# Two decoder layers over four batches: the second layer's V tiles all loaded after the next batch's first layer, and the GLU products cut in quarters

## Chip, cores and metric

The kernel runs on one core of a Trainium2 chip. The metric is the device time of one execution in microseconds (us). Eleven executions of the kernel before are given, and one more was taken with the profiler.

## The reference

The program computes the same two blocks twice, with the same weights and the same caches: an attention block over a cached K and V, and a gated feed-forward block (GLU). Four batches (b = 0 to 3) hold one query token each.

```python
# B=4, Sq=1, D=512; Hq=32 query heads, Hkv=8 cached heads, Sk=4096, Dh=128; F=1792
def _A_ref(x, k_cache, v_cache, wq, wo):
    q = (x @ wq) as heads; k, v = caches, each head used by 4 query heads
    p = softmax(q @ k^T * Dh ** -0.5)
    return (p @ v) @ wo
def _B_ref(x, w_gate, w_up, w_down):
    return (sigmoid(x @ w_gate) * (x @ w_up)) @ w_down

x = A_x
x = x + _A_ref(_layernorm(x), A_k_cache, A_v_cache, A_wq, A_wo)      # layer 0
x = x + _B_ref(_layernorm(x), B_w_gate, B_w_up, B_w_down)
x = x + _A_ref(_layernorm(x), A_k_cache, A_v_cache, A_wq, A_wo)      # layer 1
x = x + _B_ref(_layernorm(x), B_w_gate, B_w_up, B_w_down)
```

All tensors are bf16. The caches are 33.6 MB each. K is read from memory once, for both layers; V is read twice, once for each layer.

## The kernel before

**Tiles and slots.** A cached head of one batch comes as two tiles of 512 KB, q = 0 and q = 1. `K(b)` is 16 tiles, `V0(b)` the 16 tiles of V as layer 0 reads them, `V1(b)` the same 16 tiles read again for layer 1. They share a ring of 22 slots (`NS`), `ring0` to `ring21`. A V tile is free again when its 16 matmuls (`values`, O_ps) are done. A K tile stays for longer: it is transposed in place (`transpose_k`, VectorE), read by the scores of layer 0 and, after the whole feed-forward block of that batch, by the scores of layer 1. So 16 slots are held by a batch's K until layer 1's scores are done, and 6 slots carry everything else. The weights lie in their own space and are loaded once.

**Order of loads.** SyncE (SP) issues all loads in the order of the code, each when its slot is free. After batch 0's loads, it goes batch by batch, and here stands the number that the change touches:

```python
    pre = 3
    for b in range(1, B):
        for g in range(pre):
            load_v(1, b - 1, g)          # 6 tiles of V1(b-1)
        load_k(b, 0)                     # 16 tiles of K(b), in two halves
        load_k(b, 1)
        for g in range(8):
            load_v(0, b, g)              # 16 tiles of V0(b)
        for g in range(pre, 8):
            load_v(1, b - 1, g)          # the other 10 tiles of V1(b-1)
```

At the end come the 16 tiles of V1(3).

**Order of the work.** `_Sched` is a list scheduler that runs when the kernel is built. Each operation is put with an engine, an estimated duration and a priority; `place()` plays the program through with these estimates, fixes the order of each engine's instructions and gives each load the ring slot that is free earliest in that plan. On the chip each engine then follows its fixed order and waits on semaphores, and each load waits for the former user of its fixed slot.

The flow of a batch: `scores` (S_ps) and `softmax` of layer 0, in two halves s = 0, 1 of 16 query heads; `values` with V0(b) and the projection `y_proj` (Y_ps from oT and wo); `cross(0, b)`; then the queries of layer 1 (`q_proj`, M_ps from xT and wq, and `q_spread`, which writes the `qbd` tile); `scores` and `softmax` of layer 1, and after these those of layer 0 for batch b+1. `values` of V1(b-1) are put beside this.

`cross` is the feed-forward block: residual add (`xj`), layer norm, products with `wu` (Y_ps) and `wg` (G_ps), 56 matmuls each, tanh, the `hT` product, 56 matmuls with `wd`, residual add, layer norm for the next attention. `stat` is a matmul with a constant column that sums over partitions; `rstd` is such a `stat` followed by a VectorE step (L433) and a power on GpSimd (L437) that gives the scale that tanh needs. In the kernel before, `rstd` is put after all 56 `wg` matmuls. In layer 1 all four batches go through one common `cross(1, None)` at the very end.

Of the kernel before, what the change touches and what calls it, by code (L numbers as in the profile page):

```python
# [197 lines left out]
def bass_interleave_layers__gqa_block_cached__glu_gated_glu__decode_kernel(nc, A_x, A_k, A_v, A_wq, A_wo, B_x, B_wg, B_wu, B_wd, out):  # L198
# [5 lines left out]
    P = 128  # L204
    KD = D // P
# [13 lines left out]
    S = _Sched(NS)  # L219
# [3 lines left out]
    def sb(name, shape, dtype=dt.float32):  # L223
        return es.enter_context(nc.sbuf_tensor(name, list(shape), dtype))
# [9 lines left out]
    wg = sb("wg", [P, KD, F], bf)  # L234
    wu = sb("wu", [P, KD, F], bf)
    NF = F // P
# [15 lines left out]
    rs_h = cols[:, 20:24]  # L252
# [19 lines left out]
    nb = tr  # L272
# [24 lines left out]
    def mm(o, l, r, start=True, stop=True):  # L297
        return lambda e: e.matmul(o, lhsT=l, rhs=r, start=start, stop=stop)  # L298
# [61 lines left out]
    def load_wd():  # L360
        load_w("wd", wd[:], B_wd.rearrange("(c p) n -> p c n", p=P), P * NF * D * 2)
# [13 lines left out]
        load_v(0, 0, g)  # L375
    load_w("wu", wu[:], B_wu.rearrange("(k p) n -> p k n", p=P), P * KD * F * 2)
    load_wd()
    pre = 3
    for b in range(1, B):
        for g in range(pre):  # L380
            load_v(1, b - 1, g)
# [10 lines left out]
    def bcast(ap, m):  # L392
        return ap.unsqueeze(2).broadcast_to([P, ap.shape[1], m])

    def stat(c, si, nb, w, wkey, prio):
        S.put(
            "pe", mm(G_ps[:, c:c + nb], col(w), xsum[:, si:si + nb]), 0.58, prio, reads=[f"xsum{si}", wkey], writes=["G"],
        )
# [31 lines left out]
    def rstd(mult, rs, rs_key, nb, prio):  # L430
        stat(4, 4, nb, pos, "pos", prio)
        S.put(
            "dve", lambda e: e.tensor_scalar(vpe[:, 0:nb], G_ps[:, 4:4 + nb], mult, mult * eps, op0=ALU.mult, op1=ALU.add),  # L433
            0.17, prio, reads=["G"], writes=["vpe"],
        )
        S.put(
            "pool", lambda e: e.tensor_tensor(rs, vpe[:, 0:nb], mhalf[:, 0:nb], ALU.pow), 0.6, prio,  # L437
            reads=["vpe", "mhalf"], writes=[rs_key],
        )
# [122 lines left out]
        return pi  # L562

    def values(l, b, s, pi, prio, gis=range(4)):
        for gi in gis:
            for q in range(2):
                tile = V[l, b, 4 * s + gi, q]
                fns = []
                for t in range(q * HT, (q + 1) * HT):
                    def fn(e, t=t, gi=gi, tile=tile):  # L570
                        return e.matmul(  # L571
                            O_ps[:, gi * R:(gi + 1) * R], lhsT=ring[tile.slot][:, (t % HT) * DH:(t % HT + 1) * DH],
                            rhs=pt_sb[pi][:, t % 4, t // 4, gi, :], start=t == 0, stop=t == T - 1,
                        )
                    fns.append(fn)
                S.put("pe", fns, 0.57, prio, reads=[f"pt{pi}"], writes=["O"], tiles=[tile])
        c0, c1 = gis[0] * R, (gis[-1] + 1) * R
        o = (oT1[:] if l == 0 else oT2[:, :, b])[:, 16 * s + c0:16 * s + c1]
        S.put(
            "dve", lambda e: e.tensor_tensor(o, O_ps[:, c0:c1], winv[pi][:, c0:c1], ALU.mult), 0.2, prio - 1.5,  # L580
            reads=["O", f"winv{pi}"], writes=[f"oT{l}{s}{gi}" for gi in gis],
        )
# [14 lines left out]
    def cross(l, b, prio):  # L597

        last = l == 1
        nb = B if last else 1  # L600
        xres = xj[:] if last else x0[:, b, :]
        y = Y_ps[:, 0:nb * KD]
        u = Y_ps[:, 64:64 + NF * nb]
        g = G_ps[:, 64:64 + NF * nb]
        rs = rs_h[:, 0:nb]
        if last:
            x, xkey, xt = xj[:], "xj", xTj
            S.put(
                "dve", lambda e: e.tensor_tensor(xj[:], y.rearrange("p (b k) -> p b k", b=nb), xj[:], ALU.add), 0.2, prio,
                reads=["Y", "xj"], writes=["xj"],  # L610
            )
            layer_norm(x, xkey, xTj[:], "xTj", nb, prio)
            xk, xtkey = (lambda k: xTj[:, :, k]), "xTj"
        else:
            x, xkey = xj[:, b, :], "xj"
            S.put(
                "dve", lambda e: e.scalar_tensor_tensor(
                    out=x, in0=y, scalar=1.0, in1=xres, op0=ALU.mult, op1=ALU.add, accum_out=xsum[:, 0:1],
                ), 0.3, prio, reads=["Y", "x0"], writes=["xj", "xsum0"],
            )  # L620
            layer_norm(x, xkey, xT[:], "xT", 1, prio)
            xk, xtkey = (lambda k: xT[:, k:k + 1]), "xT"
        for w, key, dst, bkey in ((wg, "wg", g, "G"), (wu, "wu", u, "Y")):
            fns = []
            for f in range(NF):
                for k in range(KD):
                    fns.append(mm(
                        dst[:, f * nb:(f + 1) * nb], w[:, k, f * P:(f + 1) * P], xk(k), k == 0, k == KD - 1,
                    ))
            S.put("pe", fns, 1.85, prio, reads=[xtkey, key], writes=[bkey])  # L630
            if w is wg:
                rstd(4.0, rs, "rs_h", nb, prio)
        if last:
            S.put(
                "dve", lambda e: e.tensor_tensor(
                    gs[:].rearrange("p (f b) -> p f b", b=nb), g.rearrange("p (f b) -> p f b", b=nb),
                    rs.unsqueeze(1).broadcast_to([P, NF, nb]), ALU.mult
                ), 0.2, prio, reads=["G", "rs_h"], writes=["gs"],
            )
            S.put("act", lambda e: e.activation(gs[:], gs[:], ACTF.Tanh), 0.25, prio, reads=["gs"], writes=["gs"])  # L640
        else:
            S.put(
                "act", lambda e: e.activation(gs[:, 0:NF], g, ACTF.Tanh, scale=rs), 0.22, prio, reads=["G", "rs_h"],
                writes=["gs"],
            )
        S.put(
            "dve", lambda e: e.scalar_tensor_tensor(
                out=hT[:, 0:NF * nb], in0=gs[:, 0:NF * nb], scalar=1.0, in1=u, op0=ALU.add, op1=ALU.mult
            ), 0.2, prio, reads=["gs", "Y"], writes=["hT"],
        )  # L650
        fns = []
        for j in range(KD):
            for f in range(NF):
                fns.append(mm(
                    y.rearrange("p (b k) -> p b k", b=nb)[:, :, j], wd[:, f, j * P:(j + 1) * P],
                    hT[:, f * nb:(f + 1) * nb], f == 0, f == NF - 1,
                ))
        S.put("pe", fns, 1.85, prio, reads=["hT", "wd"], writes=["Y"])
        if not last:
            S.put(  # L660
                "dve", lambda e: e.scalar_tensor_tensor(
                    out=x, in0=y, scalar=rs, in1=x, op0=ALU.mult, op1=ALU.add, accum_out=xsum[:, 0:1],
                ), 0.3, prio, reads=["Y", "rs_h", "xj"], writes=["xj", "xsum0"],
            )
            layer_norm(x, xkey, xT[:], "xT", 1, prio)
            rstd(float(DH), rs_q[1][:, b:b + 1], f"rs_q1{b}", 1, prio)
            return
        S.put(
            "dve", lambda e: e.tensor_tensor(
                xw[:], y.rearrange("p (b k) -> p b k", b=nb), bcast(rs, KD), ALU.mult  # L670
            ), 0.2, prio, reads=["Y", "rs_h"], writes=["xw"],
        )
        S.put("dve", lambda e: e.tensor_tensor(xTj[:], xw[:], xj[:], ALU.add), 0.17, prio, reads=["xw", "xj"], writes=["xTj"])
        S.put(
            "pe", mm(M_ps[0:16, 0:P], xTj[:].rearrange("p b k -> p (b k)"), ident_b[:]), 0.3, prio, reads=["xTj", "ident_b"],
            writes=["M"],
        )
        S.put("dve", lambda e: e.tensor_copy(x16[0:16, :], M_ps[0:16, 0:P]), 0.2, prio, reads=["M"], writes=["x16"])
        S.put(
            "act", lambda e: e.dma_start(out.rearrange("b o (k p) -> (b o k) p", k=KD), x16[0:16, :]), 0.4, prio,  # L680
            reads=["x16"], writes=["out"], dma="out",
        )
# [12 lines left out]
    def attend(l, b, s, prio, u=None):  # L695
# [12 lines left out]
        writes=["x0"],  # L708
# [5 lines left out]
    for s in range(NH):  # L714
        fns = []
# [37 lines left out]
    for s in range(NH):  # L753
        for gis in (range(0, 3), range(3, 4)):
            values(1, B - 1, s, pis[1, B - 1, s], PV, gis)
            y_proj(1, s, PX, gis)
    cross(1, None, PX)
    S.put("sp", lambda e: None, 0.1, 0, reads=["out"])

# [39 lines left out]
```

## Time and profile before

| | us |
|---|---|
| median of 11 runs (lowest, highest) | 348.74 (345.34, 351.06) |
| the profiled execution, its own time | 348.01 |
| its span in the profile | 345.7 |
| TensorE busy (matmuls / weight loads) | 220.2 / 169.5 |
| VectorE busy | 138.5 |
| ScalarE busy | 52.8 |
| read from memory, mean over the span | 114.56 MB, 331 GB/s |
| granted TensorE clock, mean | 0.68 |

The span is the part of the execution between first and last instruction; 2.3 us lie around it. The profiled execution is 0.7 us below the median. Busy shares are means over stages that have different limits, so the stages have to be looked at one by one: the table of 40 slices on the page shows where the loads run at full rate and where they don't.

### The profile page before, as it was taken

To read this page: it belongs to the slowest core of one execution; us is meant where nothing else is said; L and a number is where in the kernel's file an instruction comes from. 1 tells how busy PE (TensorE), PEld (TensorE's weight loads), DVE (VectorE), ACT (ScalarE), POOL (GpSimd) and SP (SyncE) were. 2 spreads that over 40 slices of the span, in tenths; PEclk is the share of its full clock that TensorE was granted. 3 is DMA by queue.
4 is the path that set the end of the run, shared out by engine and by line. 5 is a ranking of instruction groups with operands and counts; after the bars stand their busy time and mean duration, and the time that the engine had idled before them with its cause. 6 is when DMAs were issued, how large, how long until landed. Compare 5 with 4: busy or idle time off the path is not lost.

```text
span 345.7 us, 11881 instructions
## 1 busy us (share of the span) xinstructions
PE 220.2 (64%) x5426; PEld 169.5 (49%) x5426; DVE 138.5 (40%) x341; ACT 52.8 (15%) x128; POOL 10.5 (3%) x38
## 2 busy tenths in 40 slices
PE   1322861265877568685856587786774686777876
PEld 1202551155635147675433366684351476763765
DVE  3777610000189951101579920011899501015111
ACT  1003030000033203000240320000333020002300
POOL 5000000000000000000000000000000000000001
PEclk9999999999985555555675555555855555558755
DMA  7999999999489999999499999967899999986900
GB/s 264 372 401 410 409 342 367 409 399 377 179 292 407 407 409 367 359 379 309 149 342 383 413 391 335 398 226 297 310 414 410 409 345 370 349 325 218 388 8 2
DMA packets 36897, 115.32 MB, mean 334 GB/s; under 512 B 3312, under 2 KB 9200, under 8 KB 36848
## 3 DMA queue, kind: packets, MB, share of 16 engines
q1 hardware_dynamic: 36816, 114.57, 88.1%
q8 instruction: 42, 0.69, 0.8%
q14 instruction: 7, 0.06, 0.0%
q10 hardware_dynamic: 32, 0.00, 0.0%
HBM read 114.56 MB, written 0.00 MB: 331 GB/s over the span
## 4 chain that ended last, share of the span: by engine, by line
DMA 41%; PE 27%; issue 14%; DVE 10%; SPq 7%; POOLq 0%; ACT 0%; DVEq 0%
DMA ring<-in_A_v_cache_dram 31%; PE S_ps L488 7%; PE O_ps L571 6%; PE M_ps L298 5%; PE Y_ps L298 5%; DMA wd<-in_B_w_down_dram 5%; SPq L331 5%; DVE ring L475 4%; PE G_ps L298 3%; DMA wo<-in_A_wo_dram 3%; DMA ring<-in_A_k_cache_dram 2%; SPq L347 2%; DVE ml L504 2%; DVE qbd L466 1%; PE PT_ps L298 1%
## 5 line engine op out<-in xcount | busy, mean ns | idle before, releaser
L571 PE MATMUL O_ps<-pt_sb,ring 128*128 128x4 bf16 x2048 | 67.1, 167 | 40.5 <-DMA ring<-in_A_v_cache_dram 32.0
L571 PEld LDWEIGHTS O_ps<-pt_sb,ring 128*128 128x128 bf16 x2048 | 63.5, 105 | 48.6 <-DMA ring<-in_A_v_cache_dram 22.0
L475 DVE STREAM_TRANSPOSE ring<-ring 128x1024 int32<-128x1024 int32 x64 | 75.8, 1216 | 9.9 <-DMA ring<-in_A_k_cache_dram 9.6
L488 PE MATMUL S_ps<-ring,qbd 128*16 128x512 bf16 x512 | 54.7, 580 | 11.8 <-DVE ring L475 11.8
L528 ACT ACTIVATE p_sb<-S_ps,cols 128x512 bf16<-128x512 f32 x32 | 24.6, 772 | 94.1 <-DVE cols L523 94.1
L504 DVE TENSOR_REDUCE ml<-S_ps 128x1 f32<-128x512 f32 x32 | 21.6, 673 | 37.6 <-PE S_ps L488 37.6
L580 DVE TENSOR_TENSOR oT<-O_ps,winv 128x12 bf16<-128x12 f32 (+2 forms) x29 | 4.9, 168 | 70.7 <-PE O_ps L571 70.4
L488 PEld LDWEIGHTS S_ps<-ring,qbd 128*16 128x16 bf16 x512 | 13.3, 109 | 33.5 <-issue 16.7
L298 PE MATMUL Y_ps<-oT,wo 128*128 128x1 bf16 (+1 forms) x640 | 20.3, 166 | 9.3 <-DVE oT L580 5.7
L298 PE MATMUL PT_ps<-ident_b,p_sb 128*128 128x64 bf16 x128 | 10.7, 225 | 21.4 <-ACT p_sb L528 21.2
L298 PEld LDWEIGHTS Y_ps<-oT,wo 128*128 128x128 bf16 x640 | 18.6, 104 | 11.6 <-DVE oT L580 7.0
L298 PEld LDWEIGHTS PT_ps<-ident_b,p_sb 128*128 128x128 bf16 x128 | 6.8, 114 | 28.8 <-ACT p_sb L528 26.7
L298 PE MATMUL M_ps<-xT,wq 128*128 128x1 bf16 x512 | 15.4, 166 | 7.6 <-issue 4.9
L298 PEld LDWEIGHTS M_ps<-xT,wq 128*128 128x128 bf16 x512 | 14.5, 104 | 8.4 <-issue 5.2
L437 POOL TENSOR_TENSOR cols<-cols 128x1 f32<-128x1 f32 (+1 forms) x10 | 6.4, 639 | 326.5 <-issue 218.8
L433 DVE TENSOR_SCALAR cols<-G_ps 128x1 f32<-128x1 f32 (+1 forms) x10 | 1.6, 159 | 35.9 <-PE G_ps L298 35.9
L298 PE MATMUL M_ps<-dsel,cols 128*128 128x16 f32 x64 | 14.3, 341 | 2.7 <-DVE dsel L553 2.7
L426 ACT ACTIVATE gs<-xj,cols 128x4 f32<-128x4 f32 x8 | 2.4, 297 | 82.4 <-DVE cols L424 82.4
L298 PEld LDWEIGHTS M_ps<-dsel,cols 128*128 128x128 f32 x64 | 12.8, 281 | 3.5 <-DVE dsel L553 2.8
L298 PE MATMUL G_ps<-cols 128*128 128x1 f32 (+1 forms) x40 | 11.4, 354 | 2.4 <-DVE cols L403 0.9
L547 ACT ACTIVATE pt_sb<-PT_ps 128x512 bf16<-128x512 f32 x16 | 9.6, 597 | 21.6 <-PE PT_ps L298 21.6
L298 PEld LDWEIGHTS G_ps<-cols 128*128 128x128 f32 x40 | 10.1, 311 | 2.8 <-DVE cols L403 1.1
(73 smaller groups left out, 150.1 us busy)
## 6 DMA issues: line engine op xcount, KB each, us to landing
ring<-in_A_v_cache_dram SPq DMA_DIRECT2D x128, 512.0 KB, 7.6
ring<-in_A_k_cache_dram SPq DMA_DIRECT2D x64, 512.0 KB, 11.8
wq<-in_A_wq_dram SPq DMA_DIRECT2D x4, 1024.0 KB, 12.4
wo<-in_A_wo_dram SPq DMA_DIRECT2D x4, 1024.0 KB, 11.2
wg<-in_B_w_gate_dram SPq DMA_DIRECT2D x1, 1792.0 KB, 14.0
wu<-in_B_w_up_dram SPq DMA_DIRECT2D x1, 1792.0 KB, 11.6
wd<-in_B_w_down_dram SPq DMA_DIRECT2D x1, 1792.0 KB, 16.3
x<-in_A_x_dram SPq DMA_DIRECT2D x1, 4.0 KB, 1.6
```

The lines of the kernel that those rows point to most:

```text
L298: return lambda e: e.matmul(o, lhsT=l, rhs=r, start=start, stop=stop)
L331: return e.dma_start(ring[t.slot], t.src.rearrange("(p t) d -> p (t d)", p=P)[:, q * TS:(q + 1) * TS])
L347: S.put("sp", lambda e: e.dma_start(o, i), 0.55, 0, writes=[key], dma=key, nbytes=nbytes)
L437: "pool", lambda e: e.tensor_tensor(rs, vpe[:, 0:nb], mhalf[:, 0:nb], ALU.pow), 0.6, prio,
L466: "dve", lambda e: e.tensor_tensor(dst, i0, i1, ALU.mult), 0.45, prio, reads=["M", "mask_a"],
L475: return e.transpose(v, v)
L488: return e.matmul(bank[32 * gi:32 * gi + 16, :], lhsT=qbd[u % NQB][:, gi, nn, :], rhs=kt[:, :, nn // 2, :, nn % 2], start=nn == 0, stop=nn ...
L504: "dve", lambda e, q=q: e.tensor_reduce(ml[:, q:q + 1], S_ps[banks[q]][:], AX.X, ALU.max, negate=True), 0.65,
L528: "act", lambda e, q=q: e.activation(p_sb[:, 4 * q:4 * q + 4, :].rearrange("p c x -> p (c x)"), S_ps[banks[q]][:], ACTF.Exp, bias=nbias, s ...
L547: "act", lambda e: e.activation(pt_sb[pi][:].rearrange("p q c g h -> p (q c g h)"), PT_ps[:], ACTF.Copy), 0.65,
L571: return e.matmul(O_ps[:, gi * R:(gi + 1) * R], lhsT=ring[tile.slot][:, (t % HT) * DH:(t % HT + 1) * DH], rhs=pt_sb[pi][:, t % 4, t // 4, ...
L580: "dve", lambda e: e.tensor_tensor(o, O_ps[:, c0:c1], winv[pi][:, c0:c1], ALU.mult), 0.2, prio - 1.5,
```

## The change

It has two parts. First, `pre` goes from 3 to 0: after batch b-1's work the loader goes straight to K(b), then V0(b), and then takes all 16 tiles of V1(b-1). Correspondingly `values` of V1(b-1) for s = 0 are put in one piece of 8 tiles, after V0(b)'s. Second, the products with `wg` and `wu` are put as four operations of 3, 3, 4 and 4 column blocks (12, 12, 16 and 16 matmuls) instead of one of 56, with the estimated duration in proportion, and `rstd` is put after the second quarter of `wg`.

```diff
-    pre = 3
+    pre = 0
...
     def values(l, b, s, pi, prio, gis=range(4)):
+        if not len(gis):
+            return
...
         for w, key, dst, bkey in ((wg, "wg", g, "G"), (wu, "wu", u, "Y")):
-            fns = []
-            for f in range(NF):
-                for k in range(KD):
-                    fns.append(mm(
-                        dst[:, f * nb:(f + 1) * nb], w[:, k, f * P:(f + 1) * P], xk(k), k == 0, k == KD - 1,
-                    ))
-            S.put("pe", fns, 1.85, prio, reads=[xtkey, key], writes=[bkey])
-            if w is wg:
-                rstd(4.0, rs, "rs_h", nb, prio)
+            for f0, f1 in ((0, 3), (3, 6), (6, 10), (10, NF)):
+                fns = []
+                for f in range(f0, f1):
+                    for k in range(KD):
+                        fns.append(mm(
+                            dst[:, f * nb:(f + 1) * nb], w[:, k, f * P:(f + 1) * P], xk(k), k == 0, k == KD - 1,
+                        ))
+                S.put("pe", fns, 0.033 * len(fns), prio, reads=[xtkey, key], writes=[bkey])
+                if w is wg and f1 == 6:
+                    rstd(4.0, rs, "rs_h", nb, prio)
```

The number of instructions and bytes stays as it was. The scheduler's order changes with it, on TensorE and VectorE, and so do the slots: K(1) now lies partly in `ring16` to `ring21`, and V tiles circulate through `ring10` to `ring15` and later others. The order of the built programs shows, for batches 1 to 3, these TensorE rows of `cross` and the query projection (V1 tiles of the former batch numbered 1 to 16; matmul counts after x):

```
before: tiles 1 2, stat, tile 3, wu x56, wg x56, stat(rstd), tiles 4-7, wd x56, tiles 8 9, stat, tile 10,
        wq x64, stat, q_spread, wq x64, scores
after:  tiles 1 2, stat, tile 3, wu x12, wg x24, stat(rstd), wu x28, wg x32, wu x16, tile 4, wd x56, tiles 5 6,
        stat, tile 7, wq x64, stat, tile 8, q_spread, tiles 9 10, wq x64, scores (tiles 11-16 between these)
```

On VectorE, the transposes of K(1)'s first tiles come to stand inside batch 0's `cross` and query projection: hT (L650), transpose, xj (L664), transpose, xT (L421), L424, three transposes, L433, qbd (L466), a sixth transpose. Batches 1 to 3 have no transposes there.

## The prediction

> **What bounds the kernel now.** I read the slices first, then the table by stage, then the chain of waits, then TensorE's and SP's timelines. In the slices the last rows are the DMA's busy tenths and rate:
>
> ```profile
> PE   1322861265877568685856587786774686777876
> DMA  7999999999489999999499999967899999986900
> GB/s 264 372 401 410 409 342 367 409 399 377 179 292 407 407 409 367 359 379 309 149 342 383 413 391 335 398 226 297 310 414 410 409 345 370 349 325 218 388 8 2
> ```
>
> Loads run near 409 GB/s, where a 512 KB tile takes 1.28 us, which is also the step between landings in the trace. 115.32 MB at that rate is 282 us of the 345.7; the rest is five holes: around slices 10, 19, 26 and 36, and the last two slices. SP's timeline says what a hole is, since each begins a row of loads that waited for scores:
>
> ```profile
> 94.77 11.28 SPq L331 DMA_DIRECT2D ring<-in_A_k_cache_dram  x16
> ...
> 167.44 12.83 SPq L331 DMA_DIRECT2D ring<-in_A_k_cache_dram  x16
> ...
> 241.40 10.40 SPq L331 DMA_DIRECT2D ring<-in_A_k_cache_dram  x16
> ```
>
> I call these times Q0, Q1, Q2; Q3 is 312.5, where the last V1 loads start. L1, L2, L3 are the landings of the last V0 tile of batches 1 to 3: 142.4, 216.1, 288.2. Cutting the run there (columns: stretch, length, busy PE, PEld, DVE, ACT, POOL, clock, DMA share, GB/s):
>
> ```profile
> 142.40:167.40 25.00, 18.17 (x548) 16.42 (x552) 2.42 (x15) 1.42 (x7) 1.08 (x2) 0.50 0.84 309
> 216.10:241.40 25.30, 18.41 (x560) 16.66 (x561) 2.44 (x16) 1.42 (x7) 1.08 (x2) 0.50 0.83 314
> 288.20:312.50 24.30, 18.26 (x548) 16.47 (x552) 2.43 (x16) 1.42 (x7) 1.08 (x2) 0.50 0.88 332
> 94.80:142.40 47.60, 33.36 (x704) 22.73 (x696) 30.34 (x63) 11.29 (x24) 0.00 (x0) 0.57 0.98 370
> 312.50:330.10 17.60, 12.72 (x335) 9.42 (x323) 6.44 (x23) 5.64 (x12) 0.00 (x0) 0.79 0.80 300
> 330.10:345.70 15.60, 10.79 (x338) 10.09 (x334) 2.51 (x14) 0.25 (x1) 1.01 (x1) 0.50 0.01 3
> ```
>
> So two kinds of stretch alternate. From Q to L (47.6, 48.7, 46.8 us) 32 tiles come; 3.5 us from issue to the first landing and 32 x 1.28 is 44.5, so the DMA sets it. From L to Q (25.0, 25.3, 24.3) TensorE works through values, `y_proj`, `cross` and `q_proj`; 16 tiles (20.5 us) fit there, and then the ring is full. The chain of waits shows the latter for batch 1:
>
> ```profile
> 151.01 1.71 PE O_ps L571 x64
> 152.72 0.61 PE Y_ps L298 x23
> 153.33 1.15 issue
> 154.48 1.04 PE Y_ps L298 x33
> 155.52 0.85 PE O_ps L571 x32
> ```
>
> O_ps x64 is four V1 tiles between `rstd` and the `wd` product; "issue" is TensorE waiting for nothing recorded.
>
> **What the Trainium skill says.** "Perfetto Trace Analysis", section Optimization Strategy, reads the same bubble repeating on the resource that should be saturated as a sign of too few buffers: this trace agrees, with SP waiting 39.8 us in four waits for S_ps (the K slots). "DMA: Bandwidth & Descriptors", section Anatomy of one DMA, gives about 2 us fixed per transfer; here an idle queue takes 3.5 us to its first landing, and I use 3.5. "Runtime: NRT & Kernel Launch", section Instruction fetch mechanics, says that instructions come in blocks of 256 by DMA and that this is mostly hidden; here the gaps called issue (1.15 us above, 3.28 us at 158.5) each come with a 16 KB packet on the instruction queue, so in these stretches it is not hidden.
>
> **The change part by part.**
>
> 1. Count of tiles in each stretch. Before, L to Q carries 10 tiles of V1(b-1) and 6 of V1(b). After, it carries the 16 of V1(b-1). The same number: the first K(b+1) load has a slot that the plan frees by scores, so no K comes early in batches 1 to 3. I cost this at 0; the cover is the 16 tiles themselves. The bounds are 1 us gained or lost each time, from landings that stretched to 22.6, 25.7 and 23.4 us instead of 20.5.
>
> 2. Batch 0. The hole before Q0 took 6 tiles of V1(0); now it takes 6 of K(1). Q0 to L1 then needs 26 tiles instead of 32: 6 x 1.28 = **7.7 us less**, if the DMA still sets it. Against that, softmax and scores must keep up. VectorE reaches the last transposes about 23 us after Q0, scores end about 22 us after Q0, while V0(1) starts to land at 3.5 + 10 x 1.28 = 16.3 and its seventh tile (six slots) is due 7.7 later. That is tight: I allow a loss of 1 us, offset by the 2 us that the last two V0(1) landings lost before (steps of 1.75 and 2.48 instead of 1.28, late slots). Zero net; bounds: nothing of the 7.7 lost, or 5 lost.
>
> 3. Batch 0's transposes (1.21 us each) now stand in VectorE's order inside the critical chain. V1 tiles landed at 85.8, 87.1, 88.4, 89.6, 90.9, 92.1; K(1)'s take the same places. Before, xj (L661) ran at 86.36, xT at 87.41, qbd at 90.27. After: a transpose 85.8 to 87.0 puts xj at 87.0; the next, 87.3 to 88.5, puts xT at 88.5; three more follow, the last from 91.3 to 92.5, and then qbd at 92.7. Behind qbd wait `wq` x64 on TensorE, the scores, and SP's K loads. Q0 is **2.4 us later**. Bounds 1.5 and 3.
>
> 4. `rstd` earlier. Batch 1: `wg` ended at 150.6, `wd` began at 152.6; `stat` (0.45), L433 (0.16), L437 (0.54), tanh (0.27) and hT (0.17) stood between, with tiles 4 to 7 (4 x 0.43) on TensorE beside them. After, `stat` lies among the products and the power is done while wu x28 and wg x32 run (60 x 0.03 = 1.8 us against 1.0); tanh runs under wu x16; only hT and one tile remain, so `wd` begins 1.2 us earlier. But three of the moved tiles come back later: tile 8 before `q_spread` (0.43, TensorE had 0.07 free there) and tiles 9 and 10 (0.85) where TensorE waited 0.55 for qbd, 0.66 together. The last tiles are consumed after scores, where before tiles of V1(b) stood. Net **0.5 us less per batch, 1.5 in three**. Batch 0 gains nothing: `wd` lands at 84.6, and hT was ready at 84.4. Bounds: 0 and 1.2 each.
>
> 5. The end. After Q3, 16 tiles come instead of 10. Before, TensorE was late: scores at Q3, softmax until 320.4, then 16 tiles and `y_proj` back to back; the last tile's matmuls started at 334.1, 4.0 us after the last landing at 330.1. So DMA time was partly free there. After: 3.5 + 15 x 1.28 = 22.7, plus the 2.6 us by which the ten landings overran (17.6 against 15.0), 25.3 us from Q3 to the last landing; 0.3 for the tile before it; from the last tile to the end 345.7 - 334.1 = 11.6; minus 0.4, since tanh is now held by `wu` x56 ending at 340.5 and not by L437 ending at 340.4. That is 36.8 against 345.7 - 312.5 = 33.2: **3.6 us more**. Bounds: 1.5 if the landings don't overrun, 7.7 if the old lateness stays.
>
> 6. No work: `values` in one piece (one oT instruction of 16 columns for two of 12 and 4, 0.17 us on VectorE, which is idle there); extra semaphore waits between quarters, covered by wu x28 (0.83 us against L433's 0.25 after `stat`); K slots in another order, since SP runs ahead of the landings by 1 to 15 us in Q to L.
>
> Sum: 2.4 - 7.7 - 1.5 + 3.6 = **-3.2 us**. On the profiled execution that is 348.0 - 3.2 = 344.8; its time is 0.7 below the median, so the median goes to about 345.4.
>
> **Rivals.**
>
> (a) The sum above, 345.4; own range 342 to 347.
>
> (b) Slower: in Q0 to L1 the softmax series takes over from the DMA. TensorE's new order puts the first six V0(1) tiles behind all four score blocks of K(1), so slots are not freed before the last K tile is transposed and scored. It decides from about 23.5 us after Q0: every us later stops the loads for one. If the stage keeps its 47.6, only +2.4 - 1.5 + 3.6 = +4.5 remains, 353; if it saves a third, 351. For it: DVE is busy 30.3 of 47.6 us, TensorE's clock falls to half there. Against: the first six transposes and a quarter of the scores are done early.
>
> (c) No change: the loads' gain at the start is paid back at the end, the bounds of 2, 3 and 5 fall a little worse, and `rstd` gives nothing because tiles 4 to 10 only move: 347 to 349.
>
> (d) Faster than the sum: the issue gaps in the three L to Q stretches (5.0, 5.4, 3.5 us) shrink, as the queue is emptier when V1's late tiles wait for slots. Half of them is 7 us: 339.
>
> **How the numbers follow.** A measurement of this kernel can tell about 0.5%, 1.7 us. Chances: (a) 0.50, (b) 0.20, (c) 0.18, (d) 0.12. Faster 0.62, the same 0.18, slower 0.20. The range reaches half way into (b) and (d): 340.5 to 350.5.
>
> **What would show it.** Right: K(1) transposes before the first scores of layer 1, Q0 near 97, L1 near 137, Q to L stretches of 47 afterwards, L to Q shorter by about half a us, and 36 to 37 us from Q3 to the end. Wrong: Q0 to L1 above 42 us with SP waiting for O_ps (then (b)); L to Q above 26, with TensorE waiting for a V1 landing before the scores; or issue gaps in L to Q under 3 us in all three (then (d)).

## The result: 341.5 us, 1.7% faster, and the profile after

| | before | after |
|---|---|---|
| median of the runs taken side by side (us) | 348.5 (47 runs) | 341.47 (12 runs) |
| ratio, 95% interval | | 0.9826 [0.9797, 0.9855] |
| profiled execution, its own time / span (us) | 348.01 / 345.7 | 341.92 / 339.7 |

The ratio and its interval leave out executions that were slow as a whole (over 1.5% above the fastest of the same kernel), so the ratio isn't the quotient of the medians. The forecast was 345.4 with a range of 340.5 to 350.5: the direction was right and the gain was about twice as large. The slices of the profile after are read like those of before: the last rows are the DMA's busy tenths and its rate.

```profile
PE   1332771164678695878853886889447958798476
DMA  7999999999649979978899999979999999989920
GB/s 262 379 400 410 408 345 361 409 405 373 247 153 391 408 238 411 409 281 304 292 408 410 393 352 345 388 252 332 398 407 412 373 333 416 306 301 360 403 104 2
```

Counted from 0, the hole around slice 10 is still there. Those at slices 19, 26 and 36, where the busy tenths fell to 4, 6 and 6, now show 8, 7 and 9. SP's timeline gives Q0 to Q3, the times at which loads go on that had waited for scores:

```profile
96.38 1.75 SPq L331 DMA_DIRECT2D ring<-in_A_k_cache_dram  x4
...
160.66 2.75 SPq L331 DMA_DIRECT2D ring<-in_A_k_cache_dram  x4
...
231.01 2.25 SPq L331 DMA_DIRECT2D ring<-in_A_k_cache_dram  x5
...
300.90 3.18 SPq L331 DMA_DIRECT2D ring<-in_A_v_cache_dram  x5
```

The last V0 tiles of batches 1 to 3 land at L1 = 137.6, L2 = 210.1 and L3 = 279.2. The table by stage of after (stretch, length, busy PE, PEld, DVE, ACT, POOL with counts, clock, DMA share, GB/s): first the three stretches L to Q, then the three Q to L, then Q3 to the last landing and from there to the end.

```profile
137.60:160.70 23.10, 18.29 (x559) 16.52 (x560) 2.32 (x15) 1.42 (x7) 1.08 (x2) 0.50 0.86 325
210.10:231.00 20.90, 18.09 (x548) 16.40 (x552) 2.27 (x15) 1.42 (x7) 1.08 (x2) 0.50 0.87 329
279.20:300.90 21.70, 18.15 (x548) 16.41 (x552) 2.29 (x15) 1.42 (x7) 1.08 (x2) 0.50 0.95 348
96.40:137.60 41.20, 30.42 (x603) 20.08 (x596) 23.44 (x56) 11.18 (x24) 0.00 (x0) 0.57 0.92 347
160.70:210.10 49.40, 33.18 (x704) 22.64 (x696) 30.66 (x63) 11.29 (x24) 0.00 (x0) 0.57 0.97 364
231.00:279.20 48.20, 31.95 (x708) 22.28 (x696) 30.79 (x63) 11.29 (x24) 0.00 (x0) 0.61 1.00 378
300.90:328.00 27.10, 20.39 (x546) 16.29 (x537) 6.80 (x25) 5.54 (x12) 0.00 (x0) 0.63 0.87 328
328.00:339.70 11.70, 7.46 (x219) 6.85 (x215) 2.32 (x13) 0.25 (x1) 1.01 (x1) 0.50 0.01 3
```

TensorE is busy for the same 18.1 to 18.4 us in each L to Q as before, but the stretches are shorter by 1.9, 4.4 and 2.6 us. What went is time in which TensorE did nothing. Its timeline names it; the brackets at the end hold the idle time ahead of a row and what ended it. All such gaps above 0.2 us of after's first stretch L to Q:

```profile
149.41 0.58 PE L298 MATMUL Y_ps<-hT,wd 128*128 128x1 bf16 x16 [2.38 <-issue]
...
158.47 0.30 PE L298 MATMUL M_ps<-xT,wq 128*128 128x1 bf16 x6 [1.22 <-issue]
```

Both stand in the middle of a product (x40 of the 56 `wd` matmuls had run, and x58 of the 64 `wq` ones), and the profile records no wait for an operand there. They are called issue gaps below. In the three stretches such gaps add up to 13.8 us before and 6.9 us after.

### The profile page after: what moved, and what is told of

Same layout as the page of the kernel before. It is cut to its first block, busy times and chain, and to the rows that moved or that the text cites. A ratio compares the mean times of both kernels' runs of the same rounds, so it can differ in the third digit from the quotient of the medians.

```text
span 339.7 us, 11870 instructions
## 1 busy us (share of the span) xinstructions
PE 220.3 (65%) x5426; PEld 170.1 (50%) x5426; DVE 138.5 (41%) x338; ACT 52.6 (15%) x128; POOL 10.5 (3%) x38
## 4 chain that ended last, share of the span: by engine, by line
DMA 46%; PE 27%; DVE 13%; SPq 8%; issue 4%; ACT 0%; DVEq 0%; ACTq 0%
DMA ring<-in_A_v_cache_dram 34%; DMA ring<-in_A_k_cache_dram 9%; PE S_ps L488 7%; PE O_ps L573 6%; DVE ring L475 6%; SPq L331 6%; PE Y_ps L298 6%; PE M_ps L298 4%; PE G_ps L298 3%; DMA wo<-in_A_wo_dram 3%; DVE ml L504 2%; SPq L347 2%; PE PT_ps L298 1%; DVE tr L511 1%; ACT p_sb L528 0%
## 5 line engine op out<-in xcount | busy, mean ns | idle before, releaser
L573 PEld LDWEIGHTS O_ps<-pt_sb,ring 128*128 128x128 bf16 x2048 | 62.8, 104 | 49.7 <-DMA ring<-in_A_v_cache_dram 23.0
L475 DVE STREAM_TRANSPOSE ring<-ring 128x1024 int32<-128x1024 int32 x64 | 76.7, 1222 | 14.7 <-DMA ring<-in_A_k_cache_dram 14.4
L298 PE MATMUL M_ps<-dsel,cols 128*128 128x16 f32 x64 | 15.9, 369 | 11.9 <-DVE qbd L466 9.0
L298 PE MATMUL PT_ps<-ident_b,p_sb 128*128 128x64 bf16 x128 | 11.0, 229 | 15.2 <-ACT p_sb L528 15.1
L298 PEld LDWEIGHTS M_ps<-dsel,cols 128*128 128x128 f32 x64 | 14.6, 316 | 12.4 <-DVE qbd L466 9.2
L298 PEld LDWEIGHTS PT_ps<-ident_b,p_sb 128*128 128x128 bf16 x128 | 7.6, 121 | 24.1 <-ACT p_sb L528 21.0
L536 ACT ACTIVATE p_sb<-PT_ps 128x512 bf16<-128x512 f32 x16 | 9.6, 597 | 15.1 <-PE PT_ps L298 15.1
L298 PEld LDWEIGHTS G_ps<-cols 128*128 128x128 f32 x40 | 10.1, 311 | 3.4 <-DVE cols L403 1.1
## 6 DMA issues: line engine op xcount, KB each, us to landing
wg<-in_B_w_gate_dram SPq DMA_DIRECT2D x1, 1792.0 KB, 13.8
```

The lines of the kernel that those rows point to most:

```text
L475: return e.transpose(v, v)
L536: "act", lambda e: e.activation(pt1.rearrange("p c g a h -> p (c g a h)"), PT_ps[:], ACTF.Copy), 0.65, prio,
L573: return e.matmul(O_ps[:, gi * R:(gi + 1) * R], lhsT=ring[tile.slot][:, (t % HT) * DH:(t % HT + 1) * DH], rhs=pt_sb[pi][:, t % 4, t // 4, ...
```

## The experiments

**How they were read.** A second execution of each kernel was taken, to see what of a single trace repeats. Between landings the sum can be followed without regard to when the scores end (differences of rounded times, so the last digit can be off by one):

| us | before, two executions | after, two executions | difference of the means | forecast |
|---|---|---|---|---|
| start to L1 | 142.4, 141.1 | 137.6, 137.6 | -4.2 | -5.3 |
| L1 to L2 | 73.7, 72.0 | 72.5, 72.2 | -0.5 | -0.5 |
| L2 to L3 | 72.1, 73.6 | 69.1, 69.1 | -3.8 | -0.5 |
| L3 to end | 57.6, 58.0 | 60.4, 60.7 | +2.8 | +3.1 |
| issue gaps in the three L to Q | 13.8, 15.4 | 6.9, 9.3 | -6.5 | 0 |
| issue gaps after Q3 | 0.97, 0.83 | 4.7, 5.2 | +4.1 | 0 |

The gaps are part of the stretches above them, not an addition. What exceeds the forecast lies nearly all between L2 and L3, where the gaps of L2 to Q2 fell from 5.4 and 6.8 us to 1.5 and 1.8. Three theories were set against each other. **Counts:** the gain comes from the number of tiles that stand in each stretch, as the prediction's working has it. **Blocks:** TensorE's gaps are waits for 16 KB blocks of its own instructions, which travel with the data on the same DMA engines; the change moved these gaps. **Quarters:** the cut of the GLU products, with the earlier `rstd`, is worth more than its 1.5 us.

### The second executions

Edit: none; both kernels once more.

> The kernel before once more, for a second profile, with the same question: gaps of 12 to 15.5 us in the three L to Q stretches and about 1 us after Q3 if they belong to the order; otherwise stretches that differ by more than 2 us from 25.0, 25.3 and 24.3.

> The changed kernel itself once more, for a second profile: are the issue gaps the same from execution to execution? If the gaps belong to the order of instructions and loads, the sum over the three L to Q stretches is again 5.5 to 8.5 us and the sum after Q3 4 to 5.5. If chance decides, the stretches differ by more than 2 us from 23.1, 20.9 and 21.7.

Measured: 346.96 us (span 344.7) for before and 341.93 us (span 339.6) for after. The gaps of before come again as 5.3, 6.8 and 3.4 us, with 0.8 after Q3; those of after as 5.4, 1.8 and 2.1, with 5.2. The pattern belongs to the kernel and not to the execution, with a spread of 1.6 to 2.4 us in the sum of the three. Single gaps can differ by more: the one before after's last six `wq` matmuls was 1.22 us and then 3.15.

### Each half alone

The new order of loads with the GLU products whole:

```diff
 # changed kernel
-            for f0, f1 in ((0, 3), (3, 6), (6, 10), (10, NF)):
...
+            S.put("pe", fns, 1.85, prio, reads=[xtkey, key], writes=[bkey])
+            if w is wg:
+                rstd(4.0, rs, "rs_h", nb, prio)
```

> Only the loads' half of the change: pre = 0, the GLU products whole with rstd behind them as before. Theory A (the recorded sum, loads plus quarters): loads alone are worth +2.4 - 7.7 + 3.6 = -1.7 us, so about 346.8, L to Q stretches as before (25.0, 25.3, 24.3). Theory B (the quarters spread the V1 tiles and so shrink the instruction-fetch gaps in L to Q): gaps stay near the 13.9 us of before in the three stretches, L1 some 5 us earlier, 345 to 348. Theory C (the loads alone shrink the gaps, since the loads of V1's late tiles are held back): gaps of about 7 us, near 342.

The quarters with the old order of loads:

```diff
 # kernel before, with the quarters of the changed kernel
     pre = 3
+            for f0, f1 in ((0, 3), (3, 6), (6, 10), (10, NF)):
...
```

> Only the other half: pre = 3 as before, GLU products in quarters with the early rstd. Theory A: 0.5 us in each of three L to Q stretches and 0.4 us at the end, about 346.6. Theory B: the gaps in the three L to Q stretches fall from 13.9 to about 7 us, the stretches to 22 us, and the time to about 340 to 342, since the 3.6 us at the end are not paid and neither is the later Q0. Theory C: as A, with gaps near 13.

Measured: the order of loads alone 345.65 us, ratio 0.9928 [0.9898, 0.9958]; the quarters alone 342.51 us, ratio 0.9853 [0.9811, 0.9895]. That is 2.5 and 5.1 us of 348, together 7.6, where both in one give 6.1. By the prediction's steps the order of loads should bring 1.3 (2.4 - 7.7 + 4.0, without the tail's 0.4), the quarters 1.9 (1.5 and the tail's 0.4). So the quarters brought more than twice their forecast, and on top of them the order of loads is worth 0.9 us, which the intervals don't separate from nothing. The table by stage of the quarters alone, the three L to Q:

```profile
141.10:162.60 21.50, 18.03 (x548) 16.41 (x552) 2.43 (x16) 1.42 (x7) 1.08 (x2) 0.50 0.92 326
210.70:236.20 25.50, 18.16 (x548) 16.46 (x552) 2.49 (x16) 1.42 (x7) 1.08 (x2) 0.50 0.84 311
283.30:307.70 24.40, 18.11 (x548) 16.44 (x552) 2.48 (x16) 1.42 (x7) 1.08 (x2) 0.50 0.86 318
```

Only the first is much shorter than before (25.0), and there the gaps went from 5.0 to 2.2 us; in the other two they are 4.5 and 4.8. Without the gaps the three last 59.9 us, against 60.8 before: 0.9 us for the earlier `rstd`, where 1.5 was forecast. What the quarters brought beyond it goes with a gap that shrank. With the order of loads alone the gaps in the three stretches were 3.9, 4.2 and 3.4 us, but there the stretches end earlier in the work: the first K(2) load was issued at 159.8, before layer 1's scores began at 162.1, and gaps of 1.4 and 1.9 us stand 8 and 10 us after Q1 and Q2. From L1 to the end they add up to 15.3 us with the order of loads alone and 13.1 with the quarters alone, against 14.8 and 16.2 before and 11.7 and 14.5 after. So the order of loads alone did not make the gaps fewer.

### Taking the data away: is a gap a wait behind loads?

In both kernels each V1 tile moves only 32 KB of its 512 KB (the first 128 of its 2,048 columns); the rest of the slot keeps what was there, so the values of layer 1 are not those of the reference. The plan was left with the old sizes, so that the order of instructions on every engine stays that of the full kernel.

```diff
-    def load_piece(src, q):
+    def load_piece(src, q, w=None):
...
-                ring[t.slot], t.src.rearrange("(p t) d -> p (t d)", p=P)[:, q * TS:(q + 1) * TS]
+                ring[t.slot][:, 0:w], t.src.rearrange("(p t) d -> p (t d)", p=P)[:, q * TS:q * TS + w]
...
-            V[l, b, g, q] = load_piece(A_v[b, g], q)
+            V[l, b, g, q] = load_piece(A_v[b, g], q, DH if l == 1 else None)
```

> The kernel before with each V1 load cut to one sixteenth of its bytes (32 KB instead of 512 KB; layer 1's values are then computed from what else lies in the slot); the order of all instructions stays. It asks what the issue gaps in L to Q are. If an instruction block waits behind data in the DMA engines (theory: fetch behind loads), the gaps in the three stretches fall from 13.9 us to under 2 us in total. If a block simply takes its time to come (1 us of packet and a latency), each gap stays at 1 us or more and the total above 6 us. L to Q should then be about 20 us or about 23 us.

> The changed kernel with each V1 load cut to one sixteenth of its bytes, as was done with the kernel before (layer 1's values are computed from what else lies in the slot). With no instruction block waiting behind loads, the L to Q stretches show the quarters and the early rstd alone. The recorded step 4 expects 0.5 us less than the 18.4, 18.5 and 18.4 us of the light kernel before; if the order itself gives more than that, they are below 17. Issue gaps: none in either case if the fetch theory holds.

Measured: 326.13 us for before, 320.96 us for after. The three L to Q of the light before:

```profile
141.10:159.60 18.50, 17.61 (x548) 16.10 (x552) 2.48 (x16) 1.42 (x7) 1.08 (x2) 0.50 0.11 26
206.70:225.20 18.50, 17.69 (x561) 16.25 (x562) 2.42 (x15) 1.42 (x7) 1.08 (x2) 0.50 0.11 25
271.80:290.20 18.40, 17.53 (x548) 16.10 (x552) 2.42 (x15) 1.42 (x7) 1.08 (x2) 0.50 0.12 26
```

and of the light after:

```profile
136.90:155.10 18.20, 17.87 (x563) 16.39 (x563) 2.28 (x15) 1.42 (x7) 1.08 (x2) 0.50 0.11 26
202.70:220.70 18.00, 17.64 (x548) 16.17 (x552) 2.28 (x15) 1.42 (x7) 1.08 (x2) 0.50 0.12 27
266.80:284.80 18.00, 17.61 (x548) 16.18 (x552) 2.26 (x14) 1.42 (x7) 1.08 (x2) 0.50 0.12 27
```

With the DMA engines busy for a tenth of the time, TensorE runs these 550 matmuls without one gap above 0.2 us, in either kernel, and it is busy for 17.5 to 17.9 of the 18.0 to 18.5 us. So the same instructions in the same order lose 13.8 us to gaps when V1's bytes travel beside them, and nothing when they don't. The light kernels also show what `rstd` and its neighbours are worth with nothing in the way: 0.3, 0.5 and 0.4 us per batch.

That the missing thing is an instruction block shows in the packets. The DMA queues' table of after has one line for TensorE's blocks:

```profile
q8 instruction: 42, 0.69, 0.8%
```

42 packets, of 16 KB; TensorE's 5,426 matmuls and as many weight loads are 42.4 blocks of 256. From 120 us on, every gap above 0.2 us in every trace of this study but one ends 2.2 to 2.8 us after the start of one of them (the exception, at 248.0 in the graded run below, stands at no border of a block and is not explained). In the kernel before, the gaps of L to Q fall at matmuls 1881, 2009 and 2136 of the program, then 3030, 3158, 3413 and so on: multiples of about 127.7 apart, which with their weight loads is one block of 256 instructions. And counted from the border before, the packet that ends a gap starts 1.6 to 4.3 us later than in the light version. "Runtime: NRT & Kernel Launch" of the Trainium skill, section Instruction fetch mechanics, gives the 256 instructions and calls the fetch mostly hidden: the size agrees, and in these stretches that it is hidden holds only where the loads are light.

So a gap can be worked out: it is the time from the border before to the start of the block's packet, plus the 2.2 to 2.8 us until its instructions run, less the time that TensorE takes for the block before. Over the thirteen borders that fall in before's L to Q (one without a gap is put 127 or 128 matmuls from its neighbours), the packets start on average 3.2 and 3.4 us after the border before (two executions), 2.5 and 2.7 after the change, 0.8 and 0.5 in the light kernels; the block before takes 4.8 and 4.8 us, 4.6 and 4.7, and 4.4 and 4.4. At matmul 3413, where before loses 2.5 us, the packet starts after 4.7 us before and 1.7 after, while the block takes 4.4 and 4.7. On average the change made the packets start sooner; it did not spread TensorE's instructions.

### Shifting the borders

Matmuls of no use at the program's start move every later block border by half a block (64 matmuls and their weight loads), a quarter (32), three quarters (96) or a whole block (128).

```diff
 # changed kernel, N = 64, 128, 32, 96
+    S.put("pe", [mm(G_ps[:, 256:384], ident_b[:], ident_b[:]) for _ in range(N)], 0.01, PX,
+          reads=["ident_b"], writes=["pad"])
```

> The changed kernel with 64 unused matmuls put first on TensorE, in time in which it is idle anyway; the order of all else stays. They shift every border between instruction blocks by half a block. If the gaps depend on where a border falls in the chain (a dense piece with no wait in it gives the fetch no time), the gaps in the three L to Q stretches and after Q3 change by 2 us or more in total and the time with them, either way: 338 to 346. If they depend on how full the DMA queues are at that time alone, the time stays within 1 us of the changed kernel's 341.5.

> The changed kernel with 128 matmuls of no use (and their 128 weight loads, 256 TensorE instructions, one block of 16 KB) at the very start. Every later instruction moves by exactly one block, so that the borders of the blocks fall on the same work as without the padding. If the gaps called issue are set by where the borders fall in the work: the three stretches L to Q have again about 3.6, 1.5 and 1.9 us of gaps (sum 6 to 9.5, which is what two executions of the changed kernel showed), with 4.5 to 5 after Q3, and the time is that of the changed kernel, 341 to 342.5 us. If 64 pads changed the gaps only because any padding disturbs the run: gaps differ from the changed kernel's, the sum in the three stretches may be anything from 6 to 15, and the time 343 to 346.

> The changed kernel with 32 matmuls of no use (64 instructions, a quarter of a block) at the start. If the position of the borders decides, the gaps sit 32 matmuls earlier in the work than in the changed kernel, and their sum in the three stretches L to Q is another one than 6.9 and than the 10.1 of 64 pads; the time follows the sum of all gaps from L1 to the end (11.6 in the changed kernel: 341.5 us; 12.9 with 64 pads: 343.9), 340 to 345. If the position does not matter, 341 to 342.5 with the gaps of the changed kernel.

> The changed kernel with 96 matmuls of no use (192 instructions, three quarters of a block) at the start. As with 32: if the position of the borders decides, the gaps move by three quarters of a block and their sum from L1 to the end differs from 11.6; the time is 341.5 plus about the difference, 340 to 345; the best of the four positions (0, 32, 64, 96) is then the fastest version. If the position does not matter, 341 to 342.5.

| padding | gaps in L to Q | sum | after Q3 | all from L1 on | time (us), ratio |
|---|---|---|---|---|---|
| 0, two executions | 3.6, 1.5, 1.9; 5.4, 1.8, 2.1 | 6.9; 9.3 | 4.7; 5.2 | 11.7; 14.5 | 341.47, 0.9826 [0.9797, 0.9855] |
| 128 | 2.9, 1.5, 3.5 | 7.8 | 4.3 | 12.1 | 342.72, 0.9875 [0.9844, 0.9907] |
| 32 | 4.8, 4.4, 1.8 | 10.9 | 2.7 | 16.3 | 344.58, 0.9914 [0.9884, 0.9945] |
| 64 | 2.9, 3.3, 3.9 | 10.1 | 2.9 | 17.1 | 343.86, 0.9893 [0.9834, 0.9953] |
| 96 | 1.7, 2.6, 4.4 | 8.7 | 5.6 | 16.2 | 342.73, 0.9899 [0.9787, 1.0011] |

Where the gaps can stand is settled by this. Counted from the program's start, padding included, they come at the same matmuls whatever the padding: 1881 or 1882 with 0, 32, 64 and 96, and 5073 to 5075 in all five. They belong to a place in the stream of instructions, not to a piece of work. With 128, six of the nine gaps stand 128 or 129 later than six of the unpadded kernel's, that is at the same work, and the sums come back as expected (7.8; 4.3 is just under its 4.5).

How large they are depends on the place too, as far as one trace of each can tell. With 32, 64 and 96 some gaps stand between Q and L, where the unpadded kernel has none after L1 (2.9 us at 170.6 with 64), and from L1 on they add up to 16.2 to 17.1 us; where the borders fall on the same work as without padding (0 twice, 128) it is 11.7 to 14.5. The times fit in part: 32 is slower than none with intervals that don't meet, 128 is not told from it, and 64 and 96 have four runs each. No padding is faster than none. One reservation remains: the mean clock was 0.54 to 0.59 in most runs with padding where after has 0.59 to 0.69, so that padding isn't a shift and nothing else; but 32 is as slow in its runs at 0.67 to 0.69, and 128, with the low clock, is the faster one.

### Giving V1 tiles back to the end of the stretch

The end costs 2.9 us more than before; can it be had without? Here `pre` is 0, 0, 1 and 2 for batches 0 to 3, so that some V1 tiles stand ahead of K again and fewer are left over from batch to batch.

```diff
 # kernel before, with the quarters of the changed kernel
-    pre = 3
+    PRE = [0, 0, 1, 2]
     for b in range(1, B):
+        pre = PRE[b]
...
         if b > 0:
+            pre = PRE[b]
```

> A version meant to beat both: the changed kernel with pre = 0, 1, 2 for batches 1, 2, 3. The L to Q stretches then carry 18, 18 and 16 V tiles and 12 come after Q3, where the changed kernel has 16, 16, 16 and 16. Tile-count theory: each hole before Q is filled by two more tiles, and four tiles less after Q3 are worth 5.1 us of landings, of which 2 to 4 show: 337 to 339. Fetch theory adds: fuller queues in L to Q make the gaps longer there by 1 to 3 us, so 339 to 341.

Measured: 349.17 us, ratio 0.9999 [0.9969, 1.0029]; nothing is left of the gain, quarters and all, and both forecasts (337 to 341) were missed. From Q3 to the end it took 34.1 us, near the 33.2 of before, so the repayment at the end was indeed saved. L1 stayed at 137.7. But the three L to Q took 24.8, 26.0 and 24.4 us, and TensorE's timeline shows where; two of the gaps of the third:

```profile
299.27 0.75 PE L298 MATMUL Y_ps<-hT,wd 128*128 128x1 bf16 x22 [2.28 <-issue]
...
309.76 0.46 PE L298 MATMUL M_ps<-xT,wq 128*128 128x1 bf16 x12 [2.79 <-issue]
```

The gaps are back at 4.5, 5.6 and 5.1 us, 15.2 in all, as in the kernel before. A count of tiles could not see that. The theory of counts fell with this run as an account of L to Q; for the start (L1) and the end it holds.

### Fewer loads under way at the end

From SP's issues and the landings, after has up to 12 tiles issued and not landed after Q3 (at 310.9), before at most 8. If a block waits behind all of these, a shallower queue should let it through.

```diff
 # changed kernel, in place(), after the order is fixed
+        last = [o for o in order["sp"] if o.tile is not None][-16:]
+        for k in range(4, 16):
+            last[k].deps.append(last[k - 4])
```

> The changed kernel, with one wait more in front of each of the last sixteen V1 loads but the first four: it waits for the landing of the load four before it, so that at most four are under way after Q3, where the changed kernel's trace has up to 12 issued and not landed at 310.9 us. Nothing else moves, on any engine. If the instruction blocks wait behind the loads that are queued ahead of them: the gaps called issue after Q3 fall from 4.7 and 5.2 us (two executions) to under 2.5, the loads still follow each other by 1.28 to 1.5 us, and the time is 338 to 340.5 us, faster than both kernels. If a block is late because the DMA engines are busy at all, whatever the depth: the gaps stay at 4 to 5.5 us and the time at 341 to 342.5. If four are too few to keep the engines full: landings step by more than 1.5 us, the last one comes later than 28 us after Q3, and the time is 342.5 to 345 in spite of fewer gaps.

TensorE's gaps after Q3, first in the changed kernel and then in this one, where the three added lines shift the line numbers:

```profile
309.25 0.29 PE L298 MATMUL PT_ps<-p_sb,ident_b 128*32 128x128 bf16 x7 [0.91 <-issue]
...
316.46 0.67 PE L573 MATMUL O_ps<-pt_sb,ring 128*128 128x4 bf16 x19 [2.01 <-issue]
...
322.75 2.16 PE L573 MATMUL O_ps<-pt_sb,ring 128*128 128x4 bf16 x68 [1.81 <-issue]
```

```profile
311.25 0.29 PE L301 MATMUL PT_ps<-p_sb,ident_b 128*32 128x128 bf16 x7 [1.25 <-issue]
...
317.38 0.67 PE L576 MATMUL O_ps<-pt_sb,ring 128*128 128x4 bf16 x19 [0.91 <-issue]
...
322.84 1.53 PE L576 MATMUL O_ps<-pt_sb,ring 128*128 128x4 bf16 x52 [0.98 <-issue]
```

Measured: 343.48 us, ratio 0.9862 [0.9833, 0.9891]. The three gaps stand in front of the same work and sum to 3.1 us instead of 4.7. That is neither of the two clean outcomes: a shallower queue may take a part of the gaps, but they don't go away at four tiles, and one execution can't tell 3.1 from 4.7 and 5.2 with much force. The last landing came 28.1 us after Q3, against 27.1 and 25.5 in after's two executions, so the loads lost at least what the gaps gave. No gain in time shows.

The traces hint that four is not shallow. In the eight traces with full loads and no padding, from matmul 1754 on, a block's packet started 1.0 us after the border before on average where at most two tiles were under way at that border (30 borders, one gap, of 0.28 us), and 2.9 us where there were three or more (202 borders, 66 gaps above 0.2 us), with ten or more no later than with four. This is a count over traces; no run held the loads at two. None of the versions tried is faster than the changed kernel.

## Why the prediction was right in direction and short by half

The sum was -3.2 us; the span shrank by 6.0, and by 5.1 between the second executions. The measured 341.5 lies in the forecast's range only because the range reached half way to rival (d); the sum's own range, 342 to 347, missed it.

**Step 2, batch 0, held.** Q0 to L1 took 41.2 us, 6.4 less than the 47.6 before (5.2 less between the second executions), where 7.7 was forecast. The tightness that the step named was there and small: the seventh tile of V0(1) was issued at 120.7 and landed at 124.15, 2.94 us after the sixth. Two readings of the step were loose: the landings that it quotes with steps of 1.75 and 2.48 lost 1.7 us and not 2, and its 3.5 us from issue to first landing is that of Q1 and Q3, where at Q0 it was 4.5. Rival (b), the softmax series as the new bound, would have shown a stretch above 42 us and stays out.

**Step 3 held, with a smaller size.** The chain of waits of after shows the transposes (ring L475) between xj, xT and qbd:

```profile
87.07 0.19 DVE xj L664 x2
87.27 0.77 DVE ring L475
88.03 0.32 issue
88.35 0.19 DVE xT L421
88.54 0.06 DVE cols L424
88.60 3.59 DVE ring L475 x3
92.19 0.04 DVE cols L433
92.23 0.34 DVE qbd L466
```

xj at 87.07, xT at 88.35 and qbd at 92.23 are within half a us of the forecast 87.0, 88.5 and 92.7. Q0 came at 96.4, 1.6 us later instead of 2.4.

**Step 4 held for what it counted.** Without the gaps the three L to Q lasted 60.8 us before and 58.8 after (60.9 and 59.2 in the second executions): 1.7 to 2.0 us, forecast 1.5.

**Steps 1 and 4 failed in what they left out.** Step 1 put the stretches L to Q at 0 by counting 16 tiles against 16, with a bound of 1 us each; its silent term was that the issue gaps stay as they were. They fell by 6.9 us (6.1 in the second executions). Rival (d) had named this, with 7 us for half of the gaps (which gives 338.4, not its 339) and a chance of 0.12. Its own sign was met in two stretches of three: 3.6, 1.5 and 1.9 us, with 3 as the limit. Its reason, an emptier queue, is not shown: four tiles were under way on average in L to Q of both kernels.

**But not all of (d)'s 7 us reached the end.** Q to L grew: 49.4 and 48.2 us instead of 48.6 and 46.8, +2.2 together (+1.7 in the second executions). At Q1, Q2 and Q3 of after, SP's issues and the landings show two, three and two V1 tiles still under way, where before had none, one and none: scores ended before the tiles had landed, and the loads that had waited for scores now stood behind these. From landing to landing the excess over the forecast of L1 to L3 is 3.2 us in the first executions (-4.2 instead of -1.0), and that is the miss, less 0.5 us in batch 0.

**Step 5, the end, was right from L3 to the end (+2.9 us for +3.1), and wrong inside.** Q3 to the end took 38.8 us instead of the forecast 36.8. The forecast gave the landings a 2.6 us overrun over 22.7; they took 27.1 from Q3, an overrun of 4.4. The first tile landed 5.1 us after Q3, since two V1(2) tiles were still to land; later landings had steps of 2.52 and 2.81 us. From the last landing to the end it took 11.7 us (15.6 before), so the transfer had become the bound, as the step said. Gaps of 4.7 us now stand after Q3; but at 325.5, after the last of them, TensorE waits 0.63 us for a landing, so in this execution they lie beside the loads. In the second one no such wait is seen, and from the last landing to the end it took 13.0 us. The 0.4 us in the tail is there in kind: from the first `wg` matmul to the first `wd` one it took 3.96 us instead of 4.26. The hT product now waits for `wu` and not for the power:

```profile
332.72 1.01 POOL L437 TENSOR_TENSOR cols<-cols 128x4 f32<-128x4 f32 x1 [38.03 <-issue]
...
334.85 0.21 DVE L650 SCALAR_TENSOR_TENSOR hT<-gs,Y_ps 128x56 bf16<-128x56 f32 x1 [0.71 <-PE Y_ps L298]
335.11 1.57 PEld L298 LDWEIGHTS Y_ps<-hT,wd 128*128 128x128 bf16 x56 [0.46 <-DVE hT L650]
```

Step 6's small edits show nowhere.

**What stays open.** That the gaps are waits for blocks which come late beside loads is shown, and so is that this change makes them smaller in L to Q, by packets that start sooner. Why they start sooner is not: the place of the borders has a part in it (padding), and at most four loads under way changed little, but no run here gives a gap's size ahead of time.

## What to carry to other kernels

Where the chain says "issue" in the middle of a product, look for 16 KB packets on the instruction queue: the block that TensorE needs may stand behind your own loads, and a reordering of either can move the cost. Such a gap is a term of the sum like any other, with both its ends to be bounded; to count it as unchanged because the work is unchanged is to guess. When a stage ends earlier, read from one landing to the next, since the time gained in one stretch can be the waiting of the next.

## What was not expected of the hardware

With DMA engines 83 to 88% busy in L to Q, TensorE stood for 13.8 us of 345.7 waiting for instruction blocks, and for none in the same stretches with the engines at 11 to 12%. The packet of a block takes about 1 us in both; what grows is the time until it starts. The loss is uneven: at some borders nothing, at others up to 3.3 us (3.6 in the second execution). The largest in L to Q of the kernel before, in the first:

```profile
161.81 0.67 PE L298 MATMUL M_ps<-xT,wq 128*128 128x1 bf16 x20 [3.28 <-issue]
```
